# New issue order in a fused attention and MLP-mixer kernel: GpSimd constants first, later casts behind copies, order lists searched anew

## The chip, the cores and the metric

The kernel runs on one core of one Trainium2 chip. The metric is device time in microseconds (us), the median of several executions, with lowest and highest in brackets. TensorE (PE) does matmuls and transposes, and its weight loads (PEld) overlap them (from 100 to 287.8 us in the profile before PE is busy 187.73 us with matmuls and, in the same 187.80 us, 102.11 us with weight loads); VectorE (DVE), ScalarE (ACT) and GpSimd (POOL) do the rest. SyncE (SP) and GpSimd start DMA transfers. Each execution also reports its mean granted TensorE clock, 1.0 at full speed.

## The reference, cut to what matters

Batch 8, 8 heads, 576 tokens, head size 64, float32 in and out.

```python
scores = where((rel >= 0) & (rel < 128), q @ k.T / 8 - slope[h] * abs(rel), -1e9)
attn   = softmax(scores)
x      = concat_heads(attn @ v)                     # (8, 576, 512)
u      = x + (relu(x.T @ w_tok1) @ w_tok2).T        # token mixing 576 -> 256 -> 576
out    = u + relu(u @ w_ch1) @ w_ch2                # channel mixing 512 -> 1536 -> 512
```

## The kernel before

The kernel issues its work in hand-made orders: each short name is one piece of work, and every engine executes its own part of the pieces in the order of the list (in the profile before, DVE's first `qT` copy, whose input was there at 5.1 us, ran at 8.83, behind a cast that waited for its load until 8.46). A prime means the next batch. `PROLOGUE` and `FIRST` cover the start and batch 0, `SECOND` batch 1, `PERIOD` batches 2 to 6, `LAST` batch 7.

```python
PROLOGUE = """
J M3 FC l23 M0 M1 W1 q0 q23 I l0 M2 cq0 W1 ck0 m0 l1 O q1 ck1 cq1 qt W3 v0 W4 A0 W3 v1 v2 s0 A1
W2 S20 v3 t0 A2 AT v4 S10 LW A3 S30 m1 S01 l01' S11 q01' p0 G1 l23' p1 G0 W1 qt' e1 S31 k0 q23'
S21 G2 H0 k1 v2' ek LC p2 A1' H1 A0' p3 u0 k2 u1 x0 v3' v4' k3 u2
"""
```

`I` and `J` make the identity and the distance table on GpSimd. `q0 q1 l0 l1` load the first two head pairs of q and k as float32 from SyncE; `cq` and `ck` cast them (DVE and ACT). The other names with q, l and v are casting loads from GpSimd, `qt` the 64 tail tokens. `G` and `H` load blocks of the channel weights, `LW` the token weights. `W1` to `W4` in a list are one to four dummy matmuls that are meant to keep PE's clock up. They must not be mixed up with `W1`, the token weight.

```python
def warm(n):                                   # dummies into psT, operands all zero
    def f():
        for _ in range(n):
            nc.tensor.matmul(psT[:, :], lhsT=zt[:, :], rhs=zt[:, None, :].broadcast_to([P, 4, P]), ...)

def put(cp, dst, bank, cs): ...                # A0..A3: PSUM -> SBUF copies after the transposes
    if b == 0 and hp < 2:                      # first two pairs: qT on DVE, kT on ACT, each in halves
        for cs in (slice(0, 2), slice(2, NC)):
            put(nc.vector.tensor_copy, qT, banks[0], cs)
            put(nc.scalar.copy, kT, banks[1], cs)

def tok2_hp(hp):                               # u of batch 0, by head pair
    ...
    if hp in U_ACT:                            # residual added by an identity matmul, copied by ACT
        for c in range(NC):
            nc.tensor.matmul(tv[:, c, :], lhsT=ident[:, :], rhs=xb[0][:, c, hc], ...)
        nc.scalar.copy(out=ub[0][:, :, hc], in_=tv)
    else:                                      # or by a DVE add
        nc.vector.tensor_tensor(out=ub[0][:, :, hc], in0=tv, in1=xb[0][:, :, hc], op=ALU.add)
# ... cut: scores, exps, masks, the product with v, token and channel mixing
```

The softmax here doesn't subtract the row's maximum and nothing guards it: scores larger than these inputs give would overflow.

## Time and profile before

| | before |
|---|---|
| time, median of 3 | 291.95 us (291.71 to 292.19) |
| span of the profiled execution (a fourth one, 292.6 us), its mean clock | 290.9 us, 0.994 |
| PE busy | 278.1 us, 96% |
| third pair's transposes (A2) start | 11.44 us |
| transposes of batch 1 (A3') start | 30.83 us |
| first channel-mixing block starts | 35.19 us, with 3 score sets of batch 1 done |
| last matmul ends | 287.73 us |

Read it as three stretches. From 35 us to 287.7 us PE is nearly always busy. After that comes only the last output. All that a new order can win easily lies before 35 us. The lines for it are in the prediction. The clock record of this trace holds one stretch at half clock before the last matmul, from 10.89 to 14.30 us, 3.41 us long (the views below are cut 0.06 us later; a "half-clock window" or "half window" below). It lowers the mean clock of the span by 0.5 x 3.41 / 290.9 = 0.006. So 0.994 is read as one such window, 0.988 as two, 0.982 as three, and 0.997 and more as none to speak of ("full clock" below): an estimate, as most executions have no profile.

### The profile page before, as it was taken

How to read it: one execution, taken by the hardware profiler on the slowest of the kernel's cores; microseconds unless marked ns; L12 is line 12 of the kernel's file. 1: busy time of each engine (PE TensorE's matmuls, PEld its weight loads, DVE VectorE, ACT ScalarE, POOL GpSimd, SP SyncE). 2: the span in 40 equal slices, each digit the busy share in tenths (PEclk: the TensorE clock that was granted, in tenths of full speed). 3: DMA queues.
4: the chain of work that ended last, by engine and by line, in shares of the span. 5: the costliest groups of instructions: out<-in, count | busy, mean ns of one | idle time of the engine just before them, and what ended most of it. 6: DMA issues, size and time to landing. Idle time of an engine off the chain costs nothing.

```text
span 290.9 us, 6418 instructions
## 1 busy us (share of the span) xinstructions
PE 278.1 (96%) x2691; PEld 154.0 (53%) x2691; DVE 178.3 (61%) x349; ACT 114.6 (39%) x177; POOL 99.7 (34%) x128
## 2 busy tenths in 40 slices
PE   7769799999999999999999999999999999999995
PEld 2448545645464555655565455644565455645544
DVE  2697577657766567657767457657666557533412
ACT  6696692038315614424432524423441533102100
POOL 8883545069407902950098004920000000000000
PEclk9799999999999999999999999999999999999999
DMA  6999999899999996996999968994803320042014
GB/s 167 161 197 196 203 178 145 120 176 144 128 183 142 171 235 99 130 162 168 167 87 159 176 160 113 138 178 136 149 2 80 103 72 2 36 108 74 0 38 144
DMA packets 148636, 38.00 MB, mean 131 GB/s; under 512 B 135808, under 2 KB 144128, under 8 KB 148608
## 3 DMA queue, kind: packets, MB, share of 16 engines
q0 software_dynamic: 103152, 17.41, 78.1%
q1 hardware_dynamic: 45456, 20.19, 30.7%
q8 instruction: 21, 0.34, 0.5%
q14 instruction: 7, 0.06, 0.1%
HBM read 35.85 MB, written 9.44 MB: 156 GB/s over the span
## 4 chain that ended last, share of the span: by engine, by line
PE 87%; DMA 9%; POOL 1%; issue 1%; DVE 1%; SPq 0%; ACT 0%
PE psM L500 28%; PE psM L548 27%; PE psM L458 4%; PE psS L307 4%; DMA qs<-in_q_dram 4%; PE psT L515 4%; PE psM L570 4%; PE psM L433 4%; DMA kT<-kn 3%; DMA qf<-in_q_dram 2%; PE psS L372 2%; PE psS L368 1%; PE psS L400 1%; PE psM L529 1%; PE psS L311 1%; PE psM L228 1%
## 5 line engine op out<-in xcount | busy, mean ns | idle before, releaser
L500 PE MATMUL psM<-utb,WC 128*128 128x512 bf16 x384 | 89.5, 379 | 0.0
L548 PE MATMUL psM<-WC,r 128*128 128x512 bf16 x372 | 87.1, 379 | 0.0
L321 ACT ACTIVATE pe<-psS 128x1024 bf16<-128x1024 f32 (+1 forms) x64 | 58.9, 973 | 48.8 <-PE psS L307 34.9
L548 PEld LDWEIGHTS <-r 128*128 128x128 bf16 x372 | 34.4, 98 | 40.7 <-issue 3.2
L500 PEld LDWEIGHTS <-WC 128*128 128x128 bf16 x384 | 35.1, 98 | 38.6 <-issue 1.1
L503 DVE TENSOR_SCALAR r<-psM 128x512 bf16<-128x512 f32 x64 | 43.3, 687 | 19.8 <-PE psM L500 19.8
L328 DVE TENSOR_TENSOR pb<-pe,masks 128x1024 bf16<-128x1024 bf16 (+1 forms) x52 | 33.0, 639 | 31.1 <-ACT pe L321 30.8
L184 POOL DMA_DIRECT2D kn<-in_k_dram x24 | 21.0, 892 | 82.7 <-DMA kT<-kn 76.0
L553 DVE TENSOR_TENSOR ob<-psM,ub 128x512 f32<-128x512 f32 x31 | 21.0, 688 | 19.3 <-PE psM L548 19.3
L506 ACT ACTIVATE r<-psM 128x512 bf16<-128x512 f32 x32 | 19.1, 602 | 30.3 <-PE psM L500 30.3
L184 POOL DMA_DIRECT2D vp<-in_v_dram x32 | 29.1, 964 | 4.8 <-DMA WC<-in_moe_w_ch_dram 4.8
L184 POOL DMA_DIRECT2D qn<-in_q_dram x24 | 21.3, 936 | 0.0
L518 ACT ACTIVATE r2t<-psT 128x384 bf16<-128x384 f32 x16 | 7.9, 494 | 32.3 <-PE psT L515 32.2
L382 DVE TENSOR_TENSOR xb<-psS,rt 128x512 bf16<-128x512 f32 x28 | 19.4, 691 | 1.0
L460 DVE TENSOR_TENSOR ub<-psM,xb 128x512 bf16<-128x512 f32 x28 | 17.8, 686 | 3.1 <-PE psM L458 3.1
L307 PE MATMUL psS<-qT,kT 64*128 64x256 bf16 x180 | 15.3, 276 | 1.1 <-DVE qT L233 0.8
L372 PE MATMUL psS<-vp,pb 128*128 128x65 bf16 x224 | 15.1, 193 | 0.0
L372 PEld LDWEIGHTS <-pb 128*128 128x128 bf16 x224 | 13.4, 97 | 3.2
L458 PE MATMUL psM<-r,W 128*128 128x512 bf16 x56 | 14.9, 380 | 0.0
L515 PEld LDWEIGHTS <-WC 128*128 128x128 bf16 x384 | 13.2, 98 | 3.1
L451 ACT ACTIVATE r<-psM 128x512 bf16<-128x512 f32 x7 | 4.2, 597 | 25.2 <-PE psM L442 25.2
L515 PE MATMUL psT<-utt,WC 128*128 128x64 bf16 x384 | 13.8, 193 | 0.0
(127 smaller groups left out, 294.2 us busy)
## 6 DMA issues: line engine op xcount, KB each, us to landing
out_dram<-ob SPq DMA_DIRECT2D x31, 256.0 KB, 2.4
vp<-in_v_dram POOLq DMA_DIRECT2D x32, 128.0 KB, 5.8
kn<-in_k_dram POOLq DMA_DIRECT2D x24, 128.0 KB, 4.4
qn<-in_q_dram POOLq DMA_DIRECT2D x24, 128.0 KB, 5.2
WC<-in_moe_w_ch_dram POOLq DMA_DIRECT2D x3, 512.0 KB, 12.1
WC<-in_moe_w_ch_dram POOLq DMA_DIRECT2D x2, 768.0 KB, 16.0
out_dram<-ob SPq DMA_DIRECT2D x10, 128.0 KB, 2.3
ks<-in_k_dram POOLq DMA_DIRECT2D x3, 256.0 KB, 7.2
```

Of the source, the lines that this page charges most:

```text
L184: nc.gpsimd.dma_start(out=dst, in_=src[b, :, c * P:(c + 1) * P, :].rearrange("h s d -> s h d"))
L307: nc.tensor.matmul(s[h][:, a * 256:(a + 1) * 256], lhsT=kT[i][r, kb, hp, :], rhs=qT[i][r, kb:kb + 2, hp, :], start=True, stop=True)
L321: nc.scalar.activation(out=e[:, h, :], in_=s[n][:, None, :] if split else t2[:, :, :], func=ACT.Exp, scale=scale)
L328: nc.vector.tensor_tensor(out=p[:, :].rearrange("p (h x) -> p h x", h=2)[:, h], in0=e[:, h, :], in1=masks[:, j, h].rearrange("p h g a x -> ...
L372: nc.tensor.matmul(ov, lhsT=prob(b, qb, h, 0), rhs=vt[:, qb, h, 0:D + 1], start=first, stop=(hh == 3))
L382: nc.vector.tensor_tensor(out=xb[b % 2][:, qb, :].rearrange("p (b h d) -> p b h d", b=2, h=4), in0=ov[:, :, :, 0:D], in1=rv[:, :, :, None] ...
L458: nc.tensor.matmul(t[:, :], lhsT=W2[:, j, c * P:(c + 1) * P], rhs=r1[b % 2][:, j, :], start=(j == 0), stop=(j == 1))
L500: nc.tensor.matmul(t[:, :], lhsT=WC1[:, cb, ht * P:(ht + 1) * P], rhs=utb[b % 2][:, :, cb, :], start=(cb == 0), stop=(cb == NCB - 1))
L503: nc.vector.tensor_scalar(out=r2[b % 2][:, ht, :], in0=t[:, :], scalar1=0.0, scalar2=None, op0=ALU.max)
L515: nc.tensor.matmul(o, lhsT=WC1[:, cb, ht * P:(ht + 1) * P], rhs=utt[(b // 2) % 2][:, cb, b % 2, :], start=(cb == 0), stop=(cb == NCB - 1))
L548: nc.tensor.matmul(t[:, :], lhsT=r2[b % 2][:, ht, c * P:(c + 1) * P], rhs=WC2[:, ht, :], start=(ht == 0), stop=(ht == NHT - 1))
L553: nc.vector.tensor_tensor(out=o[:, :], in0=t[:, :], in1=ub[b % 2][:, c, :], op=ALU.add)
```

## The change

The intent: let the float32 loads have the DMA engines first (in the profile before they moved 268 and 309 GB/s alone, from 2 to 3 and 3 to 4 us; once GpSimd's loads moved too, all together moved 155 to 172 from 5.5 to 8.5 us), get the first head pair's copies out before the second pair's casts, load batch 1's q and k ahead of a large weight block, and order everything else anew. The core of the diff:

```diff
-U_ACT = (0,)
-X_DVE = (1, 3)
+U_ACT = (0, 1, 3)
+X_DVE = (0, 1, 2)
 PROLOGUE = """
-J M3 FC l23 M0 M1 W1 q0 q23 I l0 M2 cq0 W1 ck0 m0 l1 O q1 ck1 cq1 qt W3 v0 W4 A0 W3 v1 v2 s0 A1
-W2 S20 v3 t0 A2 AT v4 S10 LW A3 S30 m1 S01 l01' S11 q01' p0 G1 l23' p1 G0 W1 qt' e1 S31 k0 q23'
-S21 G2 H0 k1 v2' ek LC p2 A1' H1 A0' p3 u0 k2 u1 x0 v3' v4' k3 u2
+l0 I W2 q0 q1 J M3 l1 ck0 M0 W3 M1 W3 W3 l23 cq0 O qt m0 A0 q23 W3 v3 v0 ck1 v1 M2 FC W1 cq1 A1
+s0 v2 S20 A2 t0 AT S10 A3 W2 S30 W2 S11 l01' v4 S01 q01' LW ex p0 G0 p1 W1 S21 m1 k0 S31 k1 q23'
+l23' A1' e1 qt' W2 v4' ek p2 u0 A0' p3 G1 k2 S00' LC G2 u1 v1'
 """
 # ... cut: FIRST, SECOND, PERIOD and LAST are new orders of the same pieces
-SPLIT = (1, 2, 3, 4)
-S_M = (0, 5, 6, 7)
+SPLIT = (1, 2)
+S_M = (0, 2, 4, 5, 6)
-k_DVE = (0, 1, 3)
-AK_DVE = (2,)
-AQ_ACT = (0, 1, 4, 5, 7)
-DVE_RELU = (0, 2, 3, 4, 5, 7, 10, 11)
+k_DVE = (2,)
+AK_DVE = (2, 3, 7)
+AQ_ACT = (1, 3, 4, 5, 7)
+DVE_RELU = (2, 3, 4, 5, 7, 8, 10, 11)
```

The capitals pick an engine or a buffer for single pieces. Two lines of code in the scores are adapted to them (cut).

More of the change, by code (lines that the diff above doesn't have):

```diff
@@ L27 @@
+l23' A1' e1 qt' W2 v4' ek p2 u0 A0' p3 G1 k2 S00' LC G2 u1 v1'
 """
 FIRST = """
-x1 v0' ex u3 A3' A2' AT' v1' Lk'' Lq'' UT x2 S00' S01' x3 Zq'' Zk'' T0 Lk''' S10' C8 v0'' v3''
-C9 Lq''' S20' v0''' S21' v4'' C3 e2 C5 S31' S11' C0 C2 S30' C4 v2'' v4''' C7 P0' C11 P2' T1 C1
-C10 C6 E0 D00 P1' D01 P3' D02 v1'' v2''' P4' K0' K1' D10 E2 U1' D11 D12 Zq''' U2' v1''' UT' X1'
-U0' D30 D20 S20'' S11'' D21 D31 D32 Zk''' E1 D22 S01'' U3' S00'' X2'
+H1 v3' k3 u2 v2' x0 u3 A3' v0' W1 H0 A2' Lk'' UT x2 x1 AT' Lq'' S20' x3 Zq'' Zk'' Lk''' T0 S10'
@@ L33 @@
+S01' v3'' v0'' Lq''' C9 v0''' S21' C11 v4'' C3 e2 S31' C0 C5 S30' C7 C8 S11' C10 E0 C1 C2 v2''
+C4 P2' v4''' C6 P3' D00 P0' P4' T1 E2 v1'' P1' D01 D02 K0' K1' D10 U1' v2''' D11 D12 U2' UT'
+Zq''' X1' U0' U3' D20 D30 S11'' S20'' v1''' D21 D31 E1 Zk''' S00'' D22 S01'' D32
 """
 SECOND = """
-X3 X0 T1 S30' S10' C3 C1 T0 C2 P0' C8 Lk''' C7 v3'' C5 S31' S21' C11 Lq''' v2''' C4 C10 C0 P4'
-v0''' v4''' C9 C6 D00 P1' v3''' P3' D01 P2' D02 v1''' K0' K1' S01'' S20'' D10 D11 D12 U2' UT'
-U0' U3' S00'' U1' X0' S11'' X2' D20 D21 E0 S21'' S10'' D22 E1 X1' E2 P0'' D30 X3' D31 D32
+T1 X2 X0 X3 S30' S31' T0 C8 C9 C7 C11 C2 P0' C5 Lk''' C3 v0''' C4 v1''' C1 S21' S10' C10 Lq'''
@@ L38 @@
+v2''' v3'' C0 P4' C6 D00 P3' D01 v3''' P1' P2' D02 K0' S20'' K1' v4''' S01'' D10 D11 D12 U1' U0'
+UT' U2' U3' X0' S21'' S11'' D20 D21 X3' S10'' S00'' E0 E1 D22 E2 X2' D30 D31 X1' D32 P0''
 """
 PERIOD = """
-C7 T0 C4 C3 C0 S31' S30' Zq'' C8 C2 Zk'' C11 C9 P1' C1 C10 P2' P3' Lk''' C6 C5 Lq''' P4' v0'''
-K0' K1' S01'' S00'' D00 v2''' v1''' D01 D02 T1 U2' U1' UT' U0' v3''' U3' D20 X2' X3' X1' D21
-P0'' D10 D11 v4''' S11'' S10'' X0' D12 D30 D22 D31 S20'' S21'' E0 E1 D32 E2
+C3 C7 Zq'' S31' S30' C10 C1 Zk'' C8 P1' C6 T1 P2' C11 P4' C2 C4 P3' C9 Lk''' v4''' C0 C5 K0'
@@ L43 @@
+S00'' K1' S01'' D00 v0''' D01 D02 U2' T0 Lq''' v1''' U1' U0' UT' U3' P0'' D20 X3' v2''' X2'
+v3''' X0' D10 X1' D21 D22 S11'' S10'' D11 D30 D31 E0 D12 D32 E1 E2 S21'' S20''
 """
 LAST = """
-C7 T1 C0 C1 C2 C9 C6 C8 C10 C11 C4 C3 T0 C5 D00 E0 D01 D10 D02 E1 D11 D20 D21 D22 E2 D12 D30 D31
+C8 C0 C3 C4 C7 C11 T1 C10 C9 T0 C6 C2 C1 C5 D00 E0 D01 D02 D10 D11 E1 D20 D12 E2 D21 D30 D31 D22
 D32
@@ L49 @@
 NPB = 9
-SPLIT = (1, 2, 3, 4)
-S_M = (0, 5, 6, 7)
+SPLIT = (1, 2)
+S_M = (0, 2, 4, 5, 6)
+S_P = ()
 x_DVE = (1, 2, 3)
-k_DVE = (0, 1, 3)
-AK_DVE = (2,)
-AQ_ACT = (0, 1, 4, 5, 7)
-DVE_RELU = (0, 2, 3, 4, 5, 7, 10, 11)
+k_DVE = (2,)
+AK_DVE = (2, 3, 7)
+AQ_ACT = (1, 3, 4, 5, 7)
+DVE_RELU = (2, 3, 4, 5, 7, 8, 10, 11)
 @with_exitstack
@@ L296, in f @@
             qrot[0] += 1
-            apart = b == 0 and j * 4 + kb in S_M
+            apart = j * 4 + kb in (S_M if b == 0 else S_P if b > 2 else ())
             t2 = None if apart else S2()
@@ L326, in g @@
                 if kb < NC - 1:
-                    for h in parts:
+                    for h in (parts if b == 0 else (slice(0, 2),)):
                         nc.vector.tensor_tensor(
```

## The prediction

> **What bounds the kernel now.** I read four views in this order: the page's slices, the busy time by stages, the waits of the first 31 us, and the chain that ended last. First the page:
>
> ```profile
> PE   7769799999999999999999999999999999999995
> PEclk9799999999999999999999999999999999999999
> DMA  6999999899999996996999968994803320042014
> ```
>
> A slice is 7.27 us. TensorE (PE) is full from the fifth slice to the last; only the first four have holes, and the second has a lower clock. The DMA engines are full there too. The stages, with busy time of PE, its weight loads, VectorE (DVE), ScalarE (ACT) and GpSimd (POOL), then clock, DMA share and GB/s:
>
> ```profile
> 4.50:8.50 4.00, 1.72 (x20) 0.88 (x20) 0.77 (x4) 1.97 (x5) 4.00 (x6) 1.00 1.08 171
> 8.50:11.00 2.50, 1.70 (x24) 0.88 (x25) 2.11 (x6) 1.22 (x3) 1.78 (x4) 0.98 1.98 156
> 11.00:14.30 3.30, 3.30 (x40) 2.00 (x40) 2.33 (x6) 2.62 (x6) 2.96 (x5) 0.50 2.33 159
> 14.30:18.60 4.30, 3.38 (x73) 2.36 (x70) 4.07 (x13) 4.26 (x9) 4.14 (x7) 1.00 1.38 194
> 18.60:31.00 12.40, 8.54 (x162) 7.34 (x160) 10.13 (x30) 7.32 (x15) 6.08 (x9) 1.00 1.40 199
> 100.00:287.80 187.80, 187.73 (x1689) 102.11 (x1686) 111.67 (x202) 59.42 (x85) 39.94 (x48) 1.00 0.85 113
> ```
>
> The last row is the main reading: from 100 us to the last matmul PE misses 0.07 us of 187.8. A full PE row alone does not prove full rate, so I look at one stretch of the chain (start, us, what):
>
> ```profile
> 254.99 7.77 PE psM L548 x36
> 262.76 0.86 PE psM L500 x4
> ```
>
> 36 matmuls of 512 columns in 7.77 us are 216 ns each, full speed. So new steady orders can win almost nothing (58 to 100 us: 41.63 busy of 42.00, so 0.37 us), and can only lose. What can be won lies before 31 us, where PE is busy 22.07 of 31.00 us, some of it with dummy matmuls, and 3.4 us of it at half clock. After PE's last matmul at 287.7 us come 3.1 us of one add and the output transfer, with the same last operation in the new order.
>
> Inside the first 31 us, the chain and two of the waits:
>
> ```profile
> 2.33 6.13 DMA qf<-in_q_dram
> 8.49 0.43 DVE qs L758
> 8.92 0.34 DVE qT L233
> 9.30 0.29 PE psS L276 x2
> ...
> 19.03 11.75 DMA qs<-in_q_dram
> 30.83 0.88 PE psM L228 x24
> ```
>
> ```profile
> DVE qs L758 <- DMA qf<-in_q_dram: 5.2, 2, 3.0
> PE psS L276 <- DVE qT L233: 2.8, 1, 2.8
> ```
>
> Two transfers carry it. The fourth fp32 load lands at 8.46; its cast stands in DVE's queue **before** the copies of the first head pair, so the first score matmul waits 2.8 us for a copy whose input was ready at 5.1. Later the last q load of batch 1 lands at 30.78. From there PE never stops again.
>
> [...] clock 0.50 from about 10.95 to 14.36[...]. [...] the SyncE loads alone move 251 to 306 KB per us from 2 to 5 us; once GpSimd's loads join, both together move about 165 (171 in the row from 4.5 us).
>
> **The change, part by part.** Names of the order lists: A0 to A3 are the transposes of q and k of a head pair and their copies, s/t/S score matmuls with exp and mask, p the product with v and its normalisation, k and u the token mixing, x its transposes, T, C and D the channel mixing; G are blocks of the first channel weight; a prime is the next batch.
>
> 1. *GpSimd makes ident first, then dist, then loads.* Memset 0.42 plus select 0.32 us (their rows) come ahead, so dist is ready near 3.0 instead of 2.2 and GpSimd's first load goes out near 2.9 instead of 2.15. Ident is ready near 1.7 instead of 4.6. Cost: nothing directly, as the first copies waited anyway. Gain: the four fp32 loads keep the DMA engines to themselves 0.75 us longer. About 350 KB of theirs were left at 4.5 us, which took until 8.46, a third of their lone speed; 0.75 us at about 275 KB/us leaves 145 KB, so the last should land near 6.9 (estimate), 1.5 us earlier.
>
> 2. *Cast of pair two behind the copies of pair one.* The A0 copies run near 5.9 instead of 8.8, the second cast near 6.9 to 7.4. But the second pair's transposes now precede the first scores, on PE and ACT. First exp: about 8.9 instead of 9.62. Scores of S20 about 9.0 instead of 10.7. So about 1 to 1.7 us here.
>
> 3. *Given back:* the remaining q heads of batch 0 move behind two tail loads (131 KB, 0.88 us from the landings 10.62 to 11.50). They landed at 10.62; I expect 11.5. The third pair's transposes stood at 11.44, so they are **not** earlier. ACT, which is full from 14.3 to 18.6 (4.26 of 4.30), has then done about 1.7 us of S20 already, and gets the mask exps M2 and a later t0 for it. I expect the first batch's exps to end 0 to 0.8 us earlier.
>
> 4. *Constants of work.* Dummy matmuls go from 15 to 23: 8 x 0.216 = 1.7 us (0.43 each at half clock), nearly all in holes; one stands in the full stage, 0.2 us. U_ACT gains two head pairs: 8 more matmuls of 128 columns, 8 x 0.055 = 0.45 us, in holes; it replaces two DVE adds of 0.69 us by ACT copies of 0.58. k_DVE loses three 0.42 us relus and gains one. DVE, busy 10.13 of 12.40 us from 18.6 to 31, so loses 2 x 0.69 + 2 x 0.42 = 2.2 us. Four normalisations of about 1.3 us each and six mask multiplies remain its chain. Walking it with these durations, the fourth normalisation ends near 26.1 instead of 26.9, and u3 ends near 28.5 instead of 29.36.
>
> 5. *Load order.* By bytes written, 4.10 MB of GpSimd loads end with the last q/k load of batch 1 before; 3.44 MB after, as one weight block (0.52 MB, 2.52 us from landing to landing) and batch 1's tails (0.9 us) go behind it. It should land near 30.8 - 3.4 = 27.4, so it **no longer sets** the start of A3'; u3 does, near 28.5. Gain: 30.83 - 28.5 = 2.3 us. One score set (S00', 0.54 us) moves into a hole ahead of it, one transpose set (0.23) and a dummy (0.22) come out behind. The next gate: the tails, the v tail and block G1 follow, landing near 31.2, where T0 needs it near 31.6; G2 lands near 33.7, where C9 stands near 33.2 and would wait 0.5 us.
>
> Before, the first ch1 block started at 35.2 with three score sets done; at the same state with four (0.55 more) that is 35.75. After: 33.7. **Sum: about 2.0 us**, some 0.1 us either way in the steady part.
>
> **The rivals.** *The load order gains nothing*: weight blocks G1 and G2 come as late as before in bytes (T0 complete at 4.16 MB against 3.70, C9 at 4.69 against 4.62), so PE could just wait at T0 or C9. For it: DMA is saturated to 50 us. Against it: G2 landed at 33.32 before and PE wanted it only at 35.2. With landings 1.5 us later than I think, the time is 291.5. *The clock*: if the extra dummies keep PE warm through 11 to 14.4 us, about 1.5 us of half-clock loss vanishes, most of it behind ACT; with an earlier u3 but G2 as a cap, 288.5. Against it: PE still has nothing to do between S20 and the third pair, about 9.6 to 11.5. *ACT becomes the bound of the prologue*, as it takes relus and adds: it was busy 7.32 of 12.40 us there, so it has room, but its queue is in order and a late exp ahead of a relu would cost up to 1 us. *A steady order that stalls*: PE's row would show gaps repeating five times; 0.3 us each would be 1.5 us, making 291.5. The operation counts in the period are unchanged, and the old order shows slack on every other engine (ACT 59 of 188 us), so I hold it unlikely.
>
> **Range and chances.** 291.95 - 2.0 = 289.9; a little for the clock gives 289.7. Eight in ten: 287.7 (all gates early, clock kept) to 291.7 (gates late). Faster by over 2% needs 5.8 us. PE lacks 8.9 us in 31, of which some 4 are the first loads and the start, and G2's landing caps the rest near 3; so 0.04. Slower by over 2% would need a new repeated stall: 0.02.
>
> **What would show it.** The fp32 cast of pair two starts near 7 us, not 8.5; the first exp near 8.9; A2's transposes at 11 to 11.5 waiting for a DMA; the qs/ks transposes of batch 1 near 28.5 released by no DMA; C9 at 33 to 34, perhaps on a weight DMA; PE busy over 99.8% after 100 us. I am wrong if A2's loads land after 12.5, if T0 or C9 waits over 1.5 us, or if the steady part has holes.

The sum: it came to 2.0 us in the head, 291.95 - 2.0 = 289.95, put there as 289.9, and with a little for the clock 289.7. On the clock the profile before shows only that PE was busy 1.65 of the 3.42 us from 7.53 to 10.95 us and that the clock was 0.51 in the 3.41 us after; that more dummies could keep it up was the author's estimate.

## The result, and the profile after

| | before | after |
|---|---|---|
| time, median of 4 in the same rounds | 292.07 us (291.71 to 292.34) | 289.74 us (289.40 to 290.12) |
| mean clock of the executions | 0.994 in the profiled one | 1.000 in all four |
| profiled span | 290.9 us | 288.3 us |
| A2 / A3' start | 11.44 / 30.83 us | 11.35 / 28.71 us |
| first channel-mixing block | 35.19 us, 3 score sets done | 33.65 us, 4 done |
| last matmul ends | 287.73 us | 285.16 us |

The ratio is 0.992 (95% interval 0.990 to 0.994). A ratio here is the mean time of one kernel's fast runs over that of the other's of the same rounds, so it is not quite the ratio of the medians quoted.

The page after, PE and DMA busy in tenths over 40 slices:

```profile
PE   8779999999999999999999999999999999999995
DMA  7999999699999996999699979996604320051004
```

PE's second slice is still at 7 as before. The page shows no clock row now: this trace holds no clock record (other profiles at full clock do print the row), so its 1.000, and perhaps that of the other three executions, rests on that. The instructions tell it instead: eight transposes take 0.64 us at 5.86 and 6.29 us, as at half clock (0.64 us at 11.44 us in the profile before, at clock 0.51), and about 0.4 us from 8.60 us on. The stages after, with the columns of the prediction's table (busy PE, PEld, DVE, ACT, POOL; clock; DMA share; GB/s):

```profile
8.50:11.00 2.50, 1.36 (x22) 0.69 (x22) 1.23 (x4) 1.97 (x6) 1.89 (x3) 1.00 1.79 165
11.00:14.30 3.30, 2.95 (x56) 1.85 (x56) 2.50 (x7) 2.47 (x6) 3.01 (x6) 1.00 2.22 164
18.60:31.00 12.40, 11.46 (x219) 9.40 (x220) 9.29 (x28) 10.24 (x21) 8.78 (x12) 1.00 1.41 198
58.00:100.00 42.00, 42.00 (x383) 22.43 (x382) 28.50 (x53) 19.21 (x25) 29.31 (x35) 1.00 1.78 159
100.00:285.20 185.20, 185.16 (x1671) 100.84 (x1669) 108.00 (x198) 59.15 (x83) 37.72 (x45) 1.00 0.86 112
```

Three things stand out. From 11 to 14.3 us the clock is full where it was 0.50: 56 matmuls instead of 40 in the same time. From 18.6 to 31 us PE is busy 11.46 us instead of 8.54. And from 58 us on it has practically no holes left (0.37 us of holes before, between 58 and 100 us).

Of the chain of waits that ended last, the start (start, us, what):

```profile
1.32 3.21 DMA qf<-in_q_dram
4.55 0.59 DVE qs L759
5.37 0.16 issue
5.53 0.49 DVE vp L693
6.03 0.56 DVE maskt L707
6.66 0.66 DVE qT L234 x2
7.72 0.84 DVE qs L759
8.60 0.64 PE psM L229 x16
...
11.96 7.19 DMA W<-in_moe_w_tok_dram
19.19 0.40 PE psM L641 x4
```

Two of the waits before 31 us (line waited for: us in total, times, longest):

```profile
PE psM L229 <- DMA qs<-in_q_dram: 1.1, 1, 1.1
PE psM L641 <- DMA W<-in_moe_w_tok_dram: 1.0, 1, 1.0
```

The chain no longer runs through a q load of 11.75 us that ends at 30.8. It runs through the token weight, which lands at 19.15, and then through ACT and PE. The only wait of PE's transposes for a q load is the 1.1 us of A2 near 11 us. The second cast (7.72) now stands behind the first pair's copies (6.66).

**Where the time came from.** Before's head has one score set less done when channel mixing starts; a set is 0.54 us, so its like-for-like start is 35.19 + 0.54 = 35.73, against 33.65 after: 2.08 us won in the head. From there to the last matmul it is 287.73 - 35.73 = 252.00 against 251.51: 0.49 us won later. Together 2.57 us, which agrees with the spans (2.6). Within the head, A2 is 0.09 us earlier, A3' 2.12, and nothing is won between A3' and channel mixing. So nearly the whole head gain arises between A2 and A3': that stretch took 19.39 us before and 17.36 after.

In that stretch two things changed together: the gate, a load ending at 30.78, went away, and so did the half-clock window. The first belongs to the change. Whether the second does, the trace cannot say.

### The profile page after: what moved, and what is told of

The parts are those of the page before. It is cut to its first block, busy times and chain, and to the rows that moved or that the text cites. A ratio compares the mean times of both kernels' runs of the same rounds, so it can differ in the third digit from the quotient of the medians.

```text
span 288.3 us, 6456 instructions
## 1 busy us (share of the span) xinstructions
PE 279.9 (97%) x2707; PEld 154.6 (54%) x2707; DVE 177.1 (61%) x348; ACT 114.9 (40%) x176; POOL 99.4 (34%) x128
## 4 chain that ended last, share of the span: by engine, by line
PE 90%; DMA 4%; ACT 2%; DVE 2%; issue 1%; POOL 1%; SPq 0%; DVEq 0%
PE psM L501 29%; PE psM L549 28%; PE psM L434 4%; PE psM L459 4%; PE psS L308 4%; PE psT L516 4%; PE psM L571 4%; DMA W<-in_moe_w_tok_dram 2%; PE psS L373 2%; PE psS L369 2%; PE psS L401 1%; DMA qf<-in_q_dram 1%; PE psM L530 1%; PE psS L312 1%; PE psM L491 1%
## 5 line engine op out<-in xcount | busy, mean ns | idle before, releaser
L554 DVE TENSOR_TENSOR ob<-psM,ub 128x512 f32<-128x512 f32 x31 | 21.4, 691 | 32.1 <-PE psM L549 31.9
L507 ACT ACTIVATE r<-psM 128x512 bf16<-128x512 f32 x32 | 19.1, 598 | 54.4 <-PE psM L501 53.8
L373 PE MATMUL psS<-vp,pb 128*128 128x65 bf16 x224 | 15.7, 193 | 0.0
L308 PE MATMUL psS<-qT,kT 64*128 64x256 bf16 x172 | 14.5, 272 | 0.3 <-ACT kT L234 0.3
L434 PE MATMUL psM<-xb,W 128*128 128x256 bf16 x112 | 13.4, 273 | 0.0
```

The costliest lines, as they stand in the source:

```text
L308: nc.tensor.matmul(s[h][:, a * 256:(a + 1) * 256], lhsT=kT[i][r, kb, hp, :], rhs=qT[i][r, kb:kb + 2, hp, :], start=True, stop=True)
L373: nc.tensor.matmul(ov, lhsT=prob(b, qb, h, 0), rhs=vt[:, qb, h, 0:D + 1], start=first, stop=(hh == 3))
L434: nc.tensor.matmul(st["t"][h][:, dh * 256:(dh + 1) * 256], lhsT=W1[:, c, dh * P:(dh + 1) * P], rhs=by_half(xb[b % 2][:, c, :])[:, h], star ...
L554: nc.vector.tensor_tensor(out=o[:, :], in0=t[:, :], in1=ub[b % 2][:, c, :], op=ALU.add)
```

## The experiments

**Theory:** the load order took the gate away and is the main gain. **Rival:** the clock window is the main gain, and then either the added dummies hold the clock, or those four executions were lucky. A smaller question is what the new later orders are worth. Every run is 5 rounds plus one profile, so 6 executions; all outputs were correct. Three batches ran. The kernel before had a median of 292.32 us in the first, 291.91 in the second (another chip) and 292.19 in the third. The third ran on the first one's chip and is compared with the first one's 11 executions of before and a single new one, so there "ratio" is not one of the same rounds.

### One half of the change at a time

*The new head alone* (`PROLOGUE`, `FIRST` and the constants for batch 0 from the new kernel, the later lists and `X_DVE`, `DVE_RELU` from the old):

```diff
 before, with
+PROLOGUE, FIRST = those of after      # + X2' at the end, which the old SECOND needs
+U_ACT, SPLIT, S_M, k_DVE, AK_DVE, AQ_ACT = those of after
```

> The changed kernel's prologue and first batch with the old kernel's later order lists. Theory 1 (the trace of the changed kernel: at 50 us it is some 1.7 us of wall time ahead, the other 0.8 us come from holes of 0.3 and 0.4 us at 67 and 88 us that the new later lists do not have): 290.3 to 290.5 us. Rival (the prediction: the later lists win about 0.1 us, all of the gain is in the first 31 us): 289.8 us.

Measured: 291.69 us (290.23 to 293.30), ratio 0.999 (0.996 to 1.002). Sorted by mean clock: 290.23 at 1.000; 291.11, 291.56, 291.81 at 0.994; 292.86 and 293.30 at 0.988 and 0.987. The same head that "won" 2 us wins nothing on average (9 of the 11 executions of before in these rounds had two or three half windows), and its time goes with the clock by over a microsecond for each half-clock window.

*The new later lists alone:*

```diff
 before, with
+SECOND, PERIOD, LAST, X_DVE, DVE_RELU = those of after
+FIRST = before's without its last piece X2'   # the new SECOND does it
```

> The old kernel's prologue and first batch with the changed kernel's later order lists. Theory 1: 291.2 us, 0.8 us faster than the kernel before. Rival (prediction): 291.9 to 292.0.

Measured: 292.34 us (291.06 to 292.66), ratio 1.000 (0.998 to 1.002). In its profile the weight loads of a score set waited once, near 87 us, for a DMA transpose:

```profile
PEld L307 <- DMA kT<-kn: 1.3, 1, 1.3
```

So the new `SECOND`, put behind the old `FIRST`, wants the transposed k of batch 2 before it is there, and 1.0 us of PE's time went into that hole in this execution, the only one profiled. In the changed kernel, with its own `FIRST`, PE has no such hole. So this run does not price the later lists.

### The load order by itself

*In the old kernel:*

```diff
-... q01' p0 G1 l23' p1 G0 W1 qt' e1 S31 k0 q23' S21 G2 ...
+... q01' p0 l23' p1 G0 W1 e1 S31 k0 q23' qt' G1 S21 G2 ...
```

> The kernel before with one change: the weight block G1 and batch 1's tail loads are issued after the last q load of batch 1 instead of ahead of it. Theory (the last q load sets where PE fills up): it lands near 27.4 instead of 30.8 us, the third and fourth transposes of batch 1 start near 29.4 (when u3 is done) without waiting for a DMA, and the time falls by 1.0 to 1.4 us to 290.7 to 291.0. Rival (the weights then come too late, PE waits at T0 or the first ch1 block instead): 291.8 to 292.1.

Measured: 291.79 us (291.26 to 292.17), ratio 0.999 (0.998 to 1.000). The profile shows the gate gone: no wait of PE for a load after 15 us but 0.4 us of one weight load. A3' starts at 30.18 instead of 30.83. What stands behind the gate in this old head is seen too: the chain that ended last runs from 11.9 to 23.7 us through ACT's exps and DVE's copies, mask multiplies and normalisations, with 0.8 us of PE among them. All six executions had one or two half-clock windows.

*Undone in the new kernel:*

```diff
-... LW ex p0 G0 p1 W1 S21 m1 k0 S31 k1 q23' l23' A1' e1 qt' W2 ... p3 G1 k2 ...
+... LW ex p0 G1 G0 p1 W1 S21 m1 k0 S31 k1 qt' q23' l23' A1' e1 W2 ... p3 k2 ...
```

> The changed kernel with G1 and batch 1's tail loads put back ahead of the last q and k loads of batch 1. Theory: these land near 30.4 instead of 27.0, the transposes wait for them, and 1.2 to 1.7 us of the gain are given back: 290.9 to 291.4. Rival (other parts carry the gain): within 0.4 us of the changed kernel's 289.7.

Measured: 291.11 us (290.46 to 291.51), ratio 0.996 (0.995 to 0.998); five executions at one half-clock window, 290.85 to 291.51, and one at full clock, 290.46. In its profile (one half window) no transpose of A3' waits for a load: it starts at 29.88, as in the head-only profile with the new load order (29.89), and A2 to channel mixing takes 23.27 us against 23.43. The gate was just hidden by the slower PE. The load order is not the whole gain, and still no answer is possible while the clock differs from run to run. So the clock came next.

### The clock

*The changed kernel again, unaltered:*

```diff
 after, no edit
```

> The changed kernel unaltered, six more executions. Theory (the clock decides): its first runs all had a mean granted clock of 1.000; the same prologue in the hybrid with the old later lists had 1.000 once and 0.987 to 0.994 five times, and ran 288.5 us against 289.4 to 291.6. So executions with clock 1.000 have spans of 287.7 to 288.4, and if some fall to 0.994 or 0.988 here these take 0.7 to 3 us more. Rival (the later lists keep it fast, the clock is a bystander): every span within 287.6 to 288.6 whatever the clock.

Measured: 291.93 us (290.58 to 292.14), ratio 0.999 (0.996 to 1.001). **The first result does not repeat.** Only one of the six executions was at full clock, two had one half window (290.58, 290.97) and three had two (291.92 to 292.14). The one at full clock took 291.94 for another reason, which its waits from 190 to 202 us show:

```profile
PE psM L501 <- DMA utb<-ub: 1.3, 1, 1.3
```

That is a DMA transpose of u which landed 8.2 us after its issue, against 4.3 to 4.7 for its like in the first profile. Also, the token weight landed 0.49 us later (19.64 instead of 19.15).

*Fourteen more dummies, in the holes that PE really has:*

```diff
-... FC W1 cq1 A1 s0 v2 S20 A2 t0 ... l01' v4 S01 q01' ... m1 k0 ...
+... FC W1 cq1 W2 A1 s0 v2 S20 W4 W1 A2 t0 ... l01' v4 W3 S01 q01' ... m1 W4 k0 ...
```

> The changed kernel with 14 more dummy matmuls, put where PE waits before 20 us (2 before the second transposes, 5 before the third, 3 before the fifth score block, 4 before the first token-mixing block). Theory (half-clock windows come from idle stretches): clock 1.000 in all executions and every time within 289.3 to 290.3. Rival (dummies only delay PE): 0.5 to 1 us slower than the changed kernel at equal clock.

Measured: 290.01 us (289.13 to 290.94), ratio 0.994 (0.992 to 0.997), in the same rounds as the 291.93 above. Five of six executions were at full clock. Repeated on the other chip:

> The changed kernel with 14 more dummies in its holes, once more, as the control at full clock for the two runs after it. Clock 0.999 or 1.000 in at least four of six executions, median 289.6 to 290.4.

Measured: 290.20 us (289.20 to 290.63), ratio 0.993 (0.991 to 0.995); all six at full clock (0.998 or more). So 11 of 12, against 1 of 6 for the unaltered kernel repeated and 4 of 4 when it was first run. Over every run whose orders are the same up to the token weights' load: 7 of 22 with 23 dummies (these ten, the new head alone and the load order undone), 20 of 24 with fourteen more (these twelve and the two runs of the next section, the last of which had a half window in three of six). So the dummies make a full clock usual, not certain. What the dummies do is seen in two stages of the profiles (columns as above). First the kernel with the fourteen, then the changed kernel in its first profile, then the kernel before at its own windows:

```profile
7.10:10.50 3.40, 2.96 (x31) 1.19 (x29) 2.05 (x9) 3.12 (x8) 3.40 (x5) 1.00 1.99 171
10.50:13.90 3.40, 3.40 (x59) 1.98 (x58) 3.29 (x8) 2.53 (x6) 3.34 (x6) 1.00 2.09 169
```

```profile
7.10:10.50 3.40, 2.25 (x26) 0.88 (x24) 2.11 (x9) 2.87 (x9) 2.79 (x4) 1.00 1.66 153
10.50:13.90 3.40, 2.55 (x44) 1.58 (x44) 2.48 (x7) 2.57 (x6) 3.30 (x6) 1.00 2.31 160
```

```profile
7.53:10.95 3.42, 1.65 (x24) 0.93 (x26) 2.07 (x6) 1.80 (x6) 2.70 (x5) 0.99 1.78 160
10.95:14.36 3.41, 3.41 (x42) 2.10 (x44) 2.44 (x7) 2.68 (x6) 3.07 (x5) 0.51 2.33 159
```

Before, a window in which PE was busy 1.65 of 3.42 us was followed by one at clock 0.51. The changed kernel is busy 2.25 and 2.55 of 3.40 in its first profile. The fourteen dummies bring these to 2.96 and 3.40. How the same head looked when it lost the clock shows in the profile of the load order undone, whose orders are the same up to there:

```profile
8.27:11.69 3.42, 1.54 (x28) 0.85 (x30) 1.50 (x4) 3.20 (x8) 2.79 (x5) 1.00 2.02 165
11.69:15.10 3.41, 3.41 (x43) 2.12 (x40) 2.63 (x7) 2.04 (x5) 2.90 (x5) 0.50 1.96 173
```

The clock record of that trace begins, with the rise to full clock, at 4.86 us; in the first profile the rise lies near 7.0 us, as its transposes show. In both records the half-clock stretch begins 6.83 us, twice 3.41, after the rise (4.86 to 11.69 here, 4.06 to 10.89 in the profile before, where the full-clock stretch after it lasts 276.48 us, 81 times 3.413). The windows here are cut in steps of 3.41 us from the rise; that busy time is judged in such steps is the author's estimate and was not shown. Cut so, PE's hole falls differently here: one window is busy only 1.54 us. Over the profiles with a clock record the rise lies between 3.93 and 6.85 us. In the eight profiles with half-clock windows in the head, the window ahead of each was busy 1.10 to 1.85 of 3.41 us, and once 2.15 (`b_load`, 13.08 to 16.49 us). No threshold is shown: windows busy 1.75 us (15 dummies, from 4.44 us) and 1.72 us (`after_again`, from 16.33 us) were followed by full clock.

*The added dummies taken out again*, 23 down to the 15 of before:

```diff
-... W3 M1 W3 W3 l23 ... A0 q23 W3 v3 ... A3 W2 S30 W2 S11 ... qt' W2 v4' ...   # FIRST: v0' W1 H0
+... W3 M1 W3 W1 l23 ... A0 q23 W2 v3 ... A3 S30 S11 ... qt' v4' ...            # FIRST: v0' H0
```

> The changed kernel with its dummies cut from 23 to the 15 of the kernel before (9 at the start, 2 after the first transposes, 4 later). Theory: mean clock 0.994 or lower in most executions, median 290.5 to 292. Rival (the dummies do nothing): 289.7, as the changed kernel.

Measured: 291.05 us (290.84 to 291.74), ratio 0.997 (0.995 to 0.999). No execution at full clock: two with one half window, three with two, one with three. Yet it is faster than the unaltered kernel in the same rounds (291.93). The three with two windows average 291.04, the unaltered kernel's three 292.03. So the count of half windows is not the whole story. Where they fall probably matters, but only profiled executions show that, and none of these three was profiled.

*Does a held clock help the old kernel?* Dummies in its holes, alone and with the new load order:

```diff
 b_warm:       ... v0 W4 A0 W4 W3 v1 ... S31 W4 k0 q23' S21 G2 H0 W2 k1 ...        # +10
 b_load_warm:  ... v0 W4 A0 W4 W4 W3 v1 ... S31 W3 k0 q23' qt' G1 S21 G2 H0 W3 k1 ... # +14, new load order
```

> The kernel before with 10 more dummies in its holes (4 more between 6.5 and 9.3 us, 4 and 2 before the first token-mixing blocks) and the old load order. Theory (the load that lands at 30.8 absorbs whatever the clock wins before it): clock mostly 1.000, time 291.0 to 291.8, at most 0.8 us below the kernel before. Rival (the clock alone explains the gain): 289.8 to 290.5.

> The kernel before with the load order changed as in the run of that alone, and 14 more dummies: 8 in the hole between 6.5 and 9.3 us, 3 each before the first two token-mixing blocks. Theory (with the last q load early, the chain of batch 0 sets the end, and it runs faster at full clock): clock 1.000 in most executions, 290.0 to 290.8. Rival (the clock costs nothing as ACT and DVE bound the prologue): 291.8, as with the load order alone.

Measured, dummies alone: 291.74 us (290.94 to 292.19), ratio 0.998 (0.997 to 1.000), two of six at full clock, so the dummies only half did their work. With the load order: 292.16 us (291.67 to 293.92), ratio 1.001 (0.999 to 1.004), four of six at full clock and **no gain even there** (mean 292.08). The second theory failed, and the first is not borne out. In the profile of the dummies alone no transpose of A3' waits for a load, and A3' starts at 29.73: the old load, issued at 18.51 instead of 19.03 us, did not absorb what was won. With the new load order too, the stretch from A2 to A3' took 18.28 us at full clock, against 18.15 in the same kernel without dummies and with two half windows. That speaks for the rival: in the old head ACT and DVE, not PE's clock, set that stretch. The dummies themselves were not in the way: they ended near 8.3 us, and PE idled 1.85 us more for a copy. A1 ran at 10.36 instead of 9.46 because the last float32 load landed at 8.93 instead of 7.99, for a reason that no run shows. It is one profile each, and the two full-clock executions of the kernel before (291.04 and 291.97) are too few to add to it.

### The load order and the fills, at full clock

With the clock held, single parts can be measured. *The load order undone in the kernel with the fourteen dummies:*

```diff
-... LW ex p0 G0 p1 ... k1 q23' l23' A1' e1 qt' W2 ... p3 G1 k2 ...
+... LW ex p0 G1 G0 p1 ... k1 qt' q23' l23' A1' e1 W2 ... p3 k2 ...
```

> The control with the load order undone (G1 and batch 1's tails ahead of the last q and k loads of batch 1). Theory (at full clock the chain of batch 0 is ready near 28 us and the late load is then what PE waits for): the load lands near 30, the third and fourth transposes wait for it some 1.5 us, time 1.2 to 1.8 us above the control. Rival (the load order is worth as little here as the half-window runs showed, 0.5 us): 0.3 to 0.7 us above it.

Measured: 290.64 us (289.87 to 291.06), ratio 0.995 (0.993 to 0.996), all six at full clock, against 290.20 for its control in the same rounds. Its waits from 20 to 35 us show the gate back:

```profile
PE psM L229 <- DMA ks<-in_k_dram: 0.9, 1, 0.9
PEld L229 <- DMA ks<-in_k_dram: 1.1, 1, 1.1
```

The last k load lands at 30.17 here. The wait is 0.9 us; the medians differ by 0.44, the means by 0.42 (95% interval -0.25 to 1.09). In the two profiles the stretch from A2 to channel mixing takes 23.37 us here and 22.15 in the control. So the new load order is worth some 0.4 us at full clock, not clear of noise, and hardly more than 1.2; the theory's 1.2 to 1.8 us is missed.

*The last suspect, ACT's fills on the new chain:* the changed kernel's chain runs through ACT from 20 to 25.7 us, with constant fills of 0.30, 0.63 and 0.41 us in it (`e1` and `ek`). `ek` was moved behind the transposes of batch 1, `e1` behind the first channel-mixing block:

```diff
-... A1' e1 qt' W2 v4' ek p2 ...          # FIRST: ... AT' Lq'' ... C9 v0''' ...
+... A1' qt' W2 v4' p2 ...                # FIRST: ... AT' ek Lq'' ... C9 e1 v0''' ...
```

> The control with three constant fills (0.43, 0.63 and 0.41 us on ACT near 22 to 23.5 us) moved behind the transposes of batch 1. Theory (the chain that ended last runs through ACT there): the copies of batch 1's first transposes and the score block behind them start 0.4 to 0.7 us earlier, time 289.3 to 289.8, 0.3 to 0.7 us below the control. Rival (DVE's fourth normalisation bounds that stretch): within 0.2 us of the control.

Measured: 290.59 us (289.78 to 292.12), ratio 0.995 (0.992 to 0.998). Three executions at full clock: 289.78, 290.05, 290.06, mean 289.96 against 290.11 of the control in the same rounds and 290.01 over its 11 at full clock. No gain is seen, but three executions cannot exclude 0.3 us (95% interval of the difference to the same rounds -0.71 to 0.41). The profile, at one half window, does show the move: A1' to A3' takes 4.86 us against 5.37 in the control, and 0.2 of these 0.5 us are lost again by the start of channel mixing. Taking 1.3 us out of the chain thus won at most a part of it: other waits stood just behind. A chain names what ended last, not what removing it brings.

### All executions by clock

Means, with the number of executions, over all sessions. Of before's first session only the profiled execution has a clock on record (292.6 us at 0.994); it is not in the table, and would bring that cell to 291.85.

| kernel | full clock | one half window | two | three |
|---|---|---|---|---|
| before | 291.50 (2) | 291.66 (4) | 292.11 (14) | 292.61 (3) |
| after | 290.19 (5) | 290.77 (2) | 292.03 (3) | none |
| after with 14 more dummies | 290.01 (11) | 290.94 (1) | none | none |

The slope is what matters. Before loses 0.2 to 0.5 us to a half window, after 0.6 to 1.3. The gate does not look like the reason that before loses less: with the gate gone (the load order in the old kernel) it is 291.72 at one window and 291.81 at two. At full clock the change gains 1.3 us (1.8 without the execution with the late transpose, (290.03 + 289.45 + 289.40 + 290.12) / 4 = 289.75, though before's two were not sifted in this way), at one window 0.9, at two nothing. Cells of two to five executions from several sessions are not more exact than some tenths. Over all ten executions of the changed kernel the mean is 290.86.

**A version that beats both in the same rounds** is therefore the changed kernel with the fourteen dummies: 290.01 against 291.93 (after) and 291.91 (before) on one chip, and 290.20 against 292.19 (before, nearly all from an earlier batch) on the other. It does not beat the changed kernel's first four (289.74); it makes their state the usual one.

## Why the prediction was right or wrong, point by point

The number was right: 289.7 predicted, 289.74 measured. The sum of 2.0 us in the head was right too (2.08). But two of its steps were wrong and offset each other, and over all ten executions the changed kernel took 289.4 to 292.1 us, which reaches past the upper end of the predicted range.

- **Right: the load order removes the gate.** Predicted: last load at 27.4, A3' at 28.5 released by no DMA. Measured: last k load at 26.99, A3' at 28.71, no DMA wait. C9 was predicted at 33.7 on G2; it started at 33.65, with G2 landed at 33.24, so just not waiting.
- **Right: the start is given back at A2.** Predicted 11 to 11.5, waiting for a DMA. Measured 11.35, after a wait of 1.1 us; the loads landed at 11.30.
- **Wrong, without effect: "First exp: about 8.9 instead of 9.62."** It came at 9.81. The float32 loads came earlier, as the step said (7.37 instead of 8.47 for the last, 6.9 predicted; GpSimd's first load went out at 2.58, not 2.9), but the second cast did not wait for its data, landed at 5.97. The A0 copies themselves ran at 6.58, not 5.9, behind a memset and two mask copies in DVE's queue (from 5.53). The cast stood behind these copies and a few memsets, started at 7.72 and took 0.83 us instead of 0.43. A2's load hides all of it.
- **Wrong: the clock step.** The prediction reckoned that the half-clock window would stay, because "PE still has nothing to do between S20 and the third pair", and that a kept clock would gain mostly behind ACT. In the profiled one of the four executions there was no such window, and the times of the other three give no sign of one. And it is not hidden: in the new head A2 to A3' takes 17.36 and 17.37 us at full clock (17.55 and 17.69 in two more profiles, 18.08 in the one whose token weight came late) and 18.3 to 18.5 us with a half window (three profiles: 18.33, 18.34, 18.48), so some 0.6 to 1.1 us. A fourth, with the fills moved, took 17.56 with a half window, as there ACT's part of the chain was shorter too.
- **Mis-sized by the same 1 us: "u3 ends near 28.5".** That walk of DVE's chain assumed the half clock. With one half window A3' starts at 29.5 to 29.9 (29.49, 29.88, 29.89 in those profiles), not 28.5. (At full clock it starts at 28.10 to 29.53, as the start of A2 shifts too; the stretch from A2 is the better measure.) The walk left out the time in which PE itself was slow. The two faults cancelled in the first session. Where one window occurred, the changed kernel took 290.77 us on average, not 289.7.
- **Mis-sized: the load order as the source of the head's gain.** The prediction put 2.3 us there. With the clock held, undoing it costs some 0.4 us (at most 1.1 by the interval, 1.2 by the profiles). The gate and PE's own pace end close together: in the profile with the load order undone, the q half of A3' ran at 28.91 and the k half at 30.21, when its load was there. So removing the one uncovers the other. The rest of the head's gain needs the full clock together with the other moves of the new head. Which of these moves carries it was not separated. The work taken off DVE is one candidate: at full clock and with the gate gone, A2 to A3' takes 18.28 us in the old head and 17.36 in the new.
- **A rival partly true.** A wait that takes the gate's place was named for T0 or C9. It came elsewhere, and small: 1.0 us of the first token-mixing matmuls for the token weight. The rival of ACT as the bound is partly true too: its busy time from 18.6 to 31 us rose from 7.32 to 10.24 us, and the chain runs through it from 20.1 to 25.6 us.
- **Too small: "some 0.1 us either way in the steady part."** From the start of channel mixing to the last matmul it gained 0.49 us against the first profile of before. The head-only run, with the new head and the old later lists, took 252.09 us there, 0.58 more than 251.51; the load-order run in the old kernel took 252.13, less 0.54 for its missing score set 251.59, only 0.08 more. So 0.1 to 0.6: PE's row now reads 42.00 of 42.00, and the old holes of 0.37 us are closed. That no engine else is the bound, and that no stall repeats, was right. The prediction's "from there PE never stops again" was not exact: before's PE was busy 26.68 of 27.00 us from 31 to 58 us, and 0.23 of that was a wait for a copy at 31.9.

**What stays open.** Why all four executions had a full clock and only one of the next six. The start of the clock record, which lies between 3.93 and 6.85 us in the profiles, may explain the two profiles compared above, by the author's estimate; whether it explains the other executions, or the session or the chip has a part, no run settles. Also open is which half window hurts how much (the 15-dummy runs), and why one DMA transpose landed late.

## What to carry to other kernels

Before believing a gain of 1%, sort the executions by their granted clock: here one kernel gave 289.4 and 292.1 us in different sessions, though its first four agreed within 0.3%. A gate that is removed gains only up to the next one behind it, and when that next one is PE's own pace, the clock becomes part of the critical path (A2 to A3' in the new head: 17.36 us at full clock, 18.3 to 18.5 with a half window in three profiles, 17.56 in the fourth, with the fills moved), and dummies in PE's real holes are worth a try (full clock in 20 of 24 executions with fourteen more, in 7 of 22 without these); where other engines set the pace, as in the old head here, a full clock won nothing (18.28 us against 18.15). Undo a part only with the clock held, or the clock is what is measured.

## What else the traces showed

- PE's longest idle stretch in the window ahead of the half-clock one was 2.77 us in the kernel before (6.53 to 9.30 us, so it began ahead of that window, which was busy 1.65 of 3.42 us). In the head-only profile a window busy 1.62 of 3.40 us was followed by one at clock 0.50. With the fourteen dummies, windows busy 2.96 and 3.40 of 3.40 us kept the clock.
- The spread of one kernel was 2.7 us (289.40 to 292.14), more than the effect under test.
- Entering and leaving the 64-row score matmuls cost about 96 and 93 ns from start to start, 0.19 us per visit, in both kernels (entries from a 512-column matmul between 60 and 230 us): 312 ns from the last 512-column matmul ahead of them to the first of them, instead of 216, and 201 ns from the last pair of them to the next matmul, instead of 108.
